# The second part's products by quarters: seven products instead of eight, with sums on GpSimd

## The chip, the cores and the metric

One NeuronCore of a Trainium2 chip runs the whole program. Its engines work in parallel, each through its own queue in a fixed order: TensorE (PE, with its weight loads shown apart as PEld), VectorE (DVE), ScalarE (ACT), GpSimd (POOL), and SyncE (SP), which here only issues DMAs. The metric is the device time of one execution in microseconds, as the median of some runs.

## The reference

Attention over chunks gives `x` (3072 tokens, 512 wide). Two dense parts follow; the change is in the second.

```python
# first part: 512 -> 2048 -> 512
h = x @ w_in
x = (np.maximum(h, 0.0) + alpha * np.minimum(h, 0.0)) @ w_out
# second part: 512 -> 1536 -> 512
a = x @ w_a
b = x @ w_b
return (a * b @ w_o2).astype(np.float32)
```

The weights arrive as 64-bit floats. Attention works on 32 queries at a time with a few neighbours and 8 memory rows for each of 8 heads.

## The kernel before

TensorE multiplies in float16. Each operand is split into a high and a low half (`split_hi` on ACT, `split_lo` on DVE), and `gemm3` makes three matmuls of each product: high by high, high by low, low by high. Each matmul loads its own 128x128 weights.

In the first part, attention units of 128 tokens feed blocks of tokens (two of 256, five of 512). Of each block, `gemm1` and `gemm2` are worked one after the other, and the result goes to DRAM as `yd`. Beside this, `chunk` turns the 64-bit words of `w_a`, `w_b` and `w_o2` into scaled halves in the tile `sp`, and stores them in DRAM (`wa_d`, `wb_d`, `w_d`): 12 chunks of 1024 columns and 8 of 768.

In the second part, `second` runs for six blocks of 512 tokens. It loads `yd`, finds the largest value (`scale`, which crosses the partitions with a small PE transpose), and splits. `one_product` makes, 12 times in a block, two products of 4 x 3 matmuls of 512 columns. ACT takes the first out of PSUM (line 1109), DVE multiplies the second by it (1114, tile `p32`) and finds its size (1120). After another `scale`, ACT and DVE split the 12 tiles (339, 343) into `phl`, and `output` makes four products of 12 x 3 matmuls of 512 columns (evacuated in line 1148, stored in 1156). So a block has 288 + 144 = 432 matmuls. `w_a`, `w_b` and `w_o2` are loaded once into the space of the first part's weights, and stay there. There are eight PSUM banks (`mm` and `mm2`, four each).

The order of all queues is fixed when the program is built. `Schedule.emit` takes, again and again, the operation that can start first by costs written in the code (`pe`, `dve`, `act`, `dma`), and among equals the one of the lowest rank. In the second part block `jb` has rank 3000 + 20 `jb`, its outputs 30 more, and what empties PSUM 1000 less. So PE works the first products of block `jb` + 1 before the outputs of block `jb`, which come while the next block's splits are made.

Of the kernel before, what the change touches and what calls it, by code (L numbers as in the profile page):

```python
# [56 lines left out]
class Schedule:  # L57
# [43 lines left out]
    def start(self, o, free):  # L101
# [3 lines left out]
        for b in o.bufs.values():  # L105
            if not b.held:
                s = b.slots
                k = need.get(id(s), 0)
                if len(s.free) <= k or (s.in_order and s.waiting[k] is not b):
                    return None  # L110
                t = max(t, s.free[k] + (self.DMA_LAG if o.engine == "SP" else 0.0))
                need[id(s)] = k + 1
        return t

    def emit(self):
# [6 lines left out]
        for _ in range(len(self.ops)):  # L122
# [25 lines left out]
            for b in o.bufs.values():  # L148
                b.users -= 1
                if not b.users and b.slots is not None:  # L150
                    b.slots.free.append(o.end + self.LAG[e])
                    b.slots.free.sort()
# [18 lines left out]
def act(n, pointers=0):  # L171
    return 0.06 + 0.09 * pointers + n * 0.833 / 1000

# [6 lines left out]
def tile_attention_moe_moe2(  # L180
# [33 lines left out]
    NC2 = DF2 // CW  # L214
    NR = DM // CR
    GR = CW // P
# [28 lines left out]
    def col(n=1):  # L245
# [14 lines left out]
    inv_w = {  # L260
        "wa": col(NC2),
        "wb": col(NC2),
        "w3": col(NR),
    }
    inv_cols = const.tile([P, NR, CR], F32, name="inv_cols")

# [6 lines left out]
        nm: dram.tile([P, n], F16, name=f"{nm}_d")  # L273
        for nm, n in (("wa", 2 * KD * DF2), ("wb", 2 * KD * DF2), ("w3", 2 * KF2 * DM))
# [21 lines left out]
    def scale(amax, s, inv, reads, writes, rank=-2000, after=()):  # L296
# [16 lines left out]
        def inverse():  # L313

            nc.vector.tensor_scalar(inv, m.tile, TINY, 1.0 / TOP, op0=ALU.max, op1=ALU.mult)
# [31 lines left out]

    xhl_slots = slots(actp, 1, [P, 2, KD, TB], F16, "xhl")
    ghl_slots = slots(actp, 1, [P, 2, KF1, TB], F16, "ghl")
    raw_slots = slots(prep, 3, [P, 1024, 2], I32, "raw")  # L350
    ah_slots = slots(prep, 1, [P, 1024], BF16, "ah", in_order=False)
    w32_slots = slots(prep, 2, [P, 1024], F32, "w32")
    sp_slots = slots(prep, 1, [P, 2, 1024], F16, "sp")

    def halves(t, kt):

        return t.rearrange("p (x k f) -> x p k f", x=2, k=kt)
# [40 lines left out]
    def chunk(nm, c, w, kt, cw, rank, load_rank):  # L398
        cols = slice(c * cw, (c + 1) * cw)
        n = kt * cw  # L400
        raw = None if nm == "w1" else Buf(raw_slots)
        rk = raw_key(c) if nm == "w1" else (raw, 0)
        ah, w32 = (None, "w32w1") if nm == "w1" else (Buf(ah_slots), Buf(w32_slots))
# [4 lines left out]
        def load():  # L408
            load_words(raw_tile(c) if nm == "w1" else raw.tile, w, kt, cols)
# [44 lines left out]
        def sizes():  # L454

            nc.scalar.activation(
                out=ah.tile[:, :n], in_=w32.tile[:, :n], func=ACTF.Abs, accum_out=am
            )
# [21 lines left out]
        if nm != "w1":  # L480
            sd.op("ACT", act(n, 2), rank, sizes, [fk], [(ah, 0), (key + "am", 0)])
# [4 lines left out]
        def scaled():  # L486
# [17 lines left out]
            else:  # L504
                sp = Buf(sp_slots)

                def hl():
                    t = sp.tile[:, :, :n]
                    return t[:, 0], t[:, 1]

                def hi_():
                    split_hi(w32.tile[:, :n], hl()[0], s)

                def lo_():
                    split_lo(w32.tile[:, :n], *hl(), s)

                def store():
                    nc.sync.dma_start(
                        out=spill[nm][:, 2 * n * c : 2 * n * (c + 1)].rearrange("p (x n) -> p x n", x=2),
                        in_=sp.tile[:, :, :n],  # L520
                    )

                sd.op("ACT", act(n, 1), rank, hi_, src, [(sp, 0)])
                sd.op("DVE", dve(n, pointers=1), rank, lo_, src + [(sp, 0)], [(sp, 1)])
                sd.op("SP", dma(n * 4 * P), rank, store, [(sp, 0), (sp, 1)], [(key, 0)])
# [416 lines left out]
    for nm, w, kt, cw in (("wa", w_a, KD, CW), ("wb", w_b, KD, CW), ("w3", w_o2, KF2, CR)):  # L942
        for c in range(w.shape[1] // cw):
            chunk(nm, c, w, kt, cw, 1000 + c, 1000 + c)


# [5 lines left out]

    late = {}

    def slots2(pool, count, shape, dtype, name, in_order=True):
        return Slots(
            count,
            lambda: pools2[pool].tile(shape, dtype, tag=name, name=name, bufs=count),
            in_order,
        )  # L960

    def w1_again():
        late["w1"] = wpool.tile([P, 2 * KD * DF1], F16, tag="w1", name="w1b")

    def w2_again():
        late["w2"] = wpool.tile([P, 2 * KF1 * DM], F16, tag="w2", name="w2b")

    sd.op("PE", 0.0, 0, w1_again, (), [(f"w1{c}", 0) for c in range(NC1)] + [("w1b", 0)])
    sd.op("PE", 0.0, 0, w2_again, (), [(f"w2{c}", 0) for c in range(NR)] + [("w2b", 0)])
    phase1 = [("att", i) for i in range(len(units))] + [  # L970
        (f"{nm}{c}", 0) for nm, n in (("wa", NC2), ("wb", NC2), ("w3", NR)) for c in range(n)
# [4 lines left out]
    n = 2 * KD * CW  # L976
    where = {}
    order = [("wa", 0), ("wb", 0), ("wa", 1), ("wb", 1)] + [("wa", c) for c in range(2, NC2)]
    for i, key in enumerate(order):
        where[key] = ("w1", i)  # L980
    for c in range(2, NC2):
# [224 lines left out]
```

## Time and profile before

| | |
|---|---|
| median of 3 runs | 1247.84 us (1247.73 to 1250.45) |
| profiled execution | 1250.38 us, of which the span is 1248.6 |
| mean granted TensorE clock | 0.997 |
| busy in the span | PE 1190.5, PEld 621.2, DVE 672.3, ACT 520.5, POOL 5.0 us |
| matmuls | 7362 recorded |

Busy time of PE is modelled: each matmul is shown longer than the distance to the next, so the distance of starts tells its pace. POOL is used only for masks at the start. In the profile's view by slices, DVE is nine tenths busy in most of the first third and two to three tenths later; PE is full from there to the end, at the full clock.

### The profile page before, as it was taken

Reading aid. Unit: us, or ns where it says so; the run is one execution under the profiler, and the core shown is the slowest. Engines: PE = TensorE matmul, PEld = TensorE weight load, DVE = VectorE, ACT = ScalarE, POOL = GpSimd, SP = SyncE. Lnnn points to the kernel's source line nnn. Section 1 sums busy time; section 2 is a strip of 40 time slices with the busy share of each in tenths; the row PEclk is TensorE's granted clock in tenths of the full one; section 3 lists DMA queues with packets and bytes.
Section 4 is the critical chain, followed back from the end, with each engine's and each line's share of the span. In section 5 each row is a group of like instructions: output and inputs, shape, how many; then the busy total and the mean of one; then the engine's idle time right before and its main releaser. Section 6 shows DMA issues by size and latency. Waiting matters only on the chain.

```text
span 1248.6 us, 18309 instructions
## 1 busy us (share of the span) xinstructions
PE 1190.5 (95%) x7362; PEld 621.2 (50%) x7362; DVE 672.3 (54%) x1225; ACT 520.5 (42%) x1204; POOL 5.0 (0%) x41
## 2 busy tenths in 40 slices
PE   4399999999999999999999999999999999999998
PEld 3278885555555544444444444444444444444443
DVE  6979998988888653252341536352342342232330
ACT  4679778866886672260450223221221221121120
POOL 1000000000000000000000000000000000000000
PEclk9999999999999999999999999999999999999999
DMA  8954776568447204101031301010000000000000
GB/s 236 267 115 101 192 187 184 143 194 238 120 123 180 66 1 113 48 1 56 12 140 64 134 1 34 1 68 1 1 34 1 1 34 1 1 35 1 1 34 34
DMA packets 157796, 99.76 MB, mean 80 GB/s; under 512 B 102912, under 2 KB 134672, under 8 KB 157712
## 3 DMA queue, kind: packets, MB, share of 16 engines
q1 hardware_dynamic: 157712, 98.59, 27.7%
q8 instruction: 58, 0.95, 0.3%
q14 instruction: 26, 0.21, 0.1%
HBM read 76.55 MB, written 22.02 MB: 79 GB/s over the span
## 4 chain that ended last, share of the span: by engine, by line
PE 76%; DVE 13%; ACT 6%; DMA 2%; issue 2%; SPq 1%; ACTq 0%; DVEq 0%
PE mm L799 24%; PE mm L801 24%; PE mm L800 24%; DVE w L443 2%; ACT sm L655 2%; PE pair L681 1%; DVE w L450 1%; DVE g L822 1%; DVE ghl L831 1%; DVE sp L343 1%; PE mm L695 1%; DVE nm L645 1%; DVE w L436 1%; DVE columns L704 1%; DVE sm L635 1%
## 5 line engine op out<-in xcount | busy, mean ns | idle before, releaser
L1109 ACT ACTIVATE t<-mm,columns 128x512 f32<-128x512 f32 x72 | 49.4, 686 | 404.8 <-PE mm L801 401.2
L1114 DVE SCALAR_TENSOR_TENSOR p<-mm,columns,t 128x512 f32<-128x512 f32 x72 | 54.0, 750 | 242.0 <-PE mm L801 234.5
L801 PE MATMUL mm<-xhl,w 128*128 128x512 f16 (+1 forms) x448 | 157.7, 352 | 1.9 <-DVE w L443 1.9
L800 PE MATMUL mm<-xhl,w 128*128 128x512 f16 (+1 forms) x448 | 157.8, 352 | 0.2 <-DVE xhl L343 0.2
L799 PE MATMUL mm<-xhl,w 128*128 128x512 f16 (+1 forms) x448 | 157.9, 352 | 0.1
L801 PE MATMUL mm<-ghl,w 128*128 128x512 f16 (+1 forms) x448 | 156.6, 350 | 0.5 <-DVE w L343 0.5
L799 PE MATMUL mm<-ghl,w 128*128 128x512 f16 (+1 forms) x448 | 156.8, 350 | 0.0
L800 PE MATMUL mm<-ghl,w 128*128 128x512 f16 (+1 forms) x448 | 156.7, 350 | 0.0
L801 PEld LDWEIGHTS <-w 128*128 128x128 f16 x896 | 88.3, 99 | 83.0 <-DVE w L443 2.2
L799 PEld LDWEIGHTS <-w 128*128 128x128 f16 x896 | 88.7, 99 | 75.5 <-issue 0.6
L800 PEld LDWEIGHTS <-w 128*128 128x128 f16 x896 | 88.3, 99 | 73.6 <-issue 0.8
L816 ACT ACTIVATE g<-mm 128x512 f32<-128x512 f32 (+1 forms) x112 | 59.9, 540 | 86.6 <-PE mm L801 83.7
L822 DVE SCALAR_TENSOR_TENSOR g<-t,columns,g 128x512 f32<-128x512 f32 (+1 forms) x112 | 74.6, 671 | 32.4 <-ACT t L819 32.1
L831 DVE TENSOR_TENSOR ghl<-g,ghl 128x512 f16<-128x512 f32 (+1 forms) x112 | 67.6, 610 | 29.8 <-ACT ghl L828 29.6
L828 ACT CAST ghl<-g 128x512 f16<-128x512 f32 (+1 forms) x112 | 62.1, 562 | 37.7 <-DVE g L822 37.5
L800 PE MATMUL mm<-w2b,w1b 128*128 128x512 f16 x192 | 72.8, 379 | 0.0
L799 PE MATMUL mm<-w2b,w1b 128*128 128x512 f16 x192 | 72.8, 379 | 0.0
L799 PE MATMUL mm<-xhl,w1b 128*128 128x512 f16 x192 | 72.8, 379 | 0.0
L801 PE MATMUL mm<-xhl,w1b 128*128 128x512 f16 x192 | 72.8, 379 | 0.0
L801 PE MATMUL mm<-w2b,w1b 128*128 128x512 f16 x192 | 72.8, 379 | 0.0
L800 PE MATMUL mm<-xhl,w1b 128*128 128x512 f16 x192 | 72.8, 379 | 0.0
L1148 DVE SCALAR_TENSOR_TENSOR g<-mm,columns,inv_cols 128x512 f32<-128x512 f32 x24 | 18.0, 748 | 100.5 <-PE mm L801 100.5
(134 smaller groups left out, 1988.4 us busy)
## 6 DMA issues: line engine op xcount, KB each, us to landing
raw<-in_moe_w_out_dram SPq DMA_DIRECT2D x8, 1024.0 KB
kw<-in_k_dram SPq DMA_DIRECT2D x40, 176.0 KB
vw<-in_v_dram SPq DMA_DIRECT2D x40, 176.0 KB
qt<-in_q_dram SPq DMA_DIRECT2D x24, 256.0 KB
raw<-in_moe_w_a_dram SPq DMA_DIRECT2D x6, 1024.0 KB
raw<-in_moe_w_b_dram SPq DMA_DIRECT2D x6, 1024.0 KB
raw<-in_moe_w_out_dram SPq DMA_DIRECT2D x8, 768.0 KB
out_dram<-g SPq DMA_DIRECT2D x24, 256.0 KB
```

What stands on the lines that cost most here:

```text
L443: nc.vector.scalar_tensor_tensor(out=f, in0=lo, scalar=29, in1=f, op0=ALU.logical_shift_right, op1=ALU.bitwise_or)
L655: nc.scalar.activation(out=sm.tile[:, o, g], in_=scored()[:, o, g], func=ACTF.Exp, bias=stat["nm"][:, i : i + 1], scale=1.0, accum_out=sta ...
L799: nc.tensor.matmul(out=ps, lhsT=lh, rhs=rh, start=first and i == 0, stop=False)
L800: nc.tensor.matmul(out=ps, lhsT=lh, rhs=rl, start=False, stop=False)
L801: nc.tensor.matmul(out=ps, lhsT=ll, rhs=rh, start=False, stop=last and i == n - 1)
L816: nc.scalar.activation(out=g.tile[:, :n], in_=ps.tile[:, :n], func=ACTF.Relu, scale=E1)
L822: nc.vector.scalar_tensor_tensor(out=g.tile[:, :n], in0=t2.tile[:, :n], scalar=nal[:, m : m + 1], in1=g.tile[:, :n], op0=ALU.mult, op1=ALU ...
L828: nc.scalar.copy(out=ghl.tile[:, 0, m, d], in_=g.tile[:, :n])
L831: nc.vector.tensor_tensor(out=ghl.tile[:, 1, m, d], in0=g.tile[:, :n], in1=ghl.tile[:, 0, m, d], op=ALU.subtract,)
L1109: nc.scalar.activation(out=a.tile, in_=pa.tile, func=ACTF.Copy, scale=iab["wa"][:, c : c + 1])
L1114: nc.vector.scalar_tensor_tensor(out=p32.tile, in0=pb.tile, scalar=iab["wb"][:, c : c + 1], in1=a.tile, op0=ALU.mult, op1=ALU.mult,)
L1148: nc.vector.scalar_tensor_tensor(out=o.tile, in0=ps.tile, scalar=io, in1=inv_cols.rearrange("p c f -> p (c f)"), op0=ALU.mult, op1=ALU.mult,)
```

## The change

The operands of the second part are cut in quarters. With two sums or differences of quarters per operand set, a product of two by two quarters takes seven products of quarters (`SEVEN`) instead of eight; the results are put together by additions. What that changes in the program:

- A unit is a block of rows by 2x2 quarters: four quarters of 256 columns and three made of them ("others"). The four sums of a unit are GpSimd instructions of 128x256 (`sums`, line 367 of the changed kernel). Then ACT and DVE split 1024 and 768 columns (`split_unit`, line 351 on DVE).
- `w_a`, `w_b` and `w_o2` are prepared in 18 units of 1024 columns; seven quarters in two halves of each are stored, 917,504 bytes.
- `pair` takes the place of two `one_product`: 2 x 7 products of 2 x 3 matmuls of 256 columns, six times in a block. `output` makes 7 products of 6 x 3 matmuls of 256 columns, twice in a block. That is 504 + 252 = 756 matmuls.
- `quarters` takes seven products out of four PSUM banks: two ACT instructions (256 and 512 columns), three on DVE (256, 512, 256; lines 409, 427, 433), and two on GpSimd (256 and 768; lines 418 and 421). DVE's 512 wait for GpSimd's 768.
- For each pair DVE multiplies 1024 columns (line 1295) and finds their size (line 1301). GpSimd makes the sums of the six units of this product and of the next block's two units of `y`.
- `w_a` and `w_b` are no longer kept. They stream through four places of a unit each (`ring_slots`): 12 units in the first block, 8 in every later one, which walks the other way.
- In the last block the sums of the product's units may go to DVE too.

```diff
+def pool(n):
+    return 0.1 + n * 2.2 / 1000
+    SEVEN = {1: (0, 0), 6: (5, 5), 5: (4, 4), 7: (2, 2), 3: (6, 3), 4: (3, 6), 2: (1, 1)}
+    def sums(rank, u, o, reads, writes, steps, cost={"POOL": pool(HT)}):
+        for out_, i, x, a, y, b, op in steps:
+            def f(e="POOL", out_=out_, i=i, x=x, a=a, y=y, b=b, op=op):
+                (nc.vector if e == "DVE" else nc.gpsimd).tensor_tensor(
+                    out=out_()[:, i], in0=x()[:, a], in1=y()[:, b], op=op
+                )
+            sd.op("POOL", cost, rank, f, reads, [(u, "sum"), (o, "sum")] + writes)
...
+        y, x, z, w = Buf(mm_slots), Buf(mm2_slots), Buf(mm2_slots), Buf(mm_slots)
+        half = {1: (y, 0), 6: (y, 1), 5: (x, 0), 7: (x, 1), 3: (z, 0), 4: (z, 1), 2: (w, 0)}
...
+        sd.op("ACT", act(HT, 1), er, first, [(y, 0)], [(c, 0)])
+        sd.op("DVE", dve(HT, pointers=1), er, add_sixth, [(y, 1), (c, 0)], [(u, 0)])
+        sd.op("ACT", act(TB, 1), er, fifth_seventh, [(x, 0), (x, 1)], [(c, 1)])
+        sd.op("POOL", pool(HT), er, c22, [(c, 1)], [(c, 3)])
+        sd.op("POOL", pool(3 * HT), er, add_all, [(u, 0)], [(c, 1), (c, 3)])
+        sd.op("DVE", dve(TB, pointers=1), er, add_third_fourth, [(z, 0), (z, 1)], [(c, 1)])
+        sd.op("DVE", dve(HT, pointers=1), er, add_second, [(w, 0)], [(c, 0)])
...
+        for j in js:
+            pair(jb, j, here, yu, ps[j], iab, amp, r)
...
+        pu = {j: Buf((ring_slots if i < 4 else yu_slots) if last_ else pu_slots) for i, j in enumerate(js)}
+        cost = {"POOL": pool(HT), "DVE": dve(HT)} if last_ else {"POOL": pool(HT)}
+        for j in js:
+            operands(r, ps[j], pu[j], lambda j=j: spj[:, j : j + 1], [(f"sp{jb}", 0), (ps[j], 0)], cost)
```

DVE's queue in the second part of the kernel before, while a middle block's products are made; the outputs named `ghl` are splits of the block before:

```order
L1114 SCALAR_TENSOR_TENSOR p32_7645<-mm2_7584,columns_84,t2_7597 128x512
L343 SCALAR_TENSOR_TENSOR ghl_7624<-p32_7276,columns_84,ghl_7624 128x512
L1120 TENSOR_REDUCE columns_84<-p32_7645 128x1
L343 SCALAR_TENSOR_TENSOR ghl_7624<-p32_7315,columns_84,ghl_7624 128x512
L1114 SCALAR_TENSOR_TENSOR p32_7667<-mm2_7630,columns_84,t2_7643 128x512
L343 SCALAR_TENSOR_TENSOR ghl_7624<-p32_7347,columns_84,ghl_7624 128x512
L1120 TENSOR_REDUCE columns_84<-p32_7667 128x1
```

The same place of DVE's queue in the changed kernel (a middle block's pairs; `cb` holds the second product, `x32_6480` and `ghl_7244` here are places of units):

```order
L409 SCALAR_TENSOR_TENSOR g_9178<-mm_9179,cb_9177 128x256
L351 SCALAR_TENSOR_TENSOR ghl_7244<-x32_6480,columns_84,ghl_7244 128x1024
L433 SCALAR_TENSOR_TENSOR cb_9177<-mm_9231,cb_9177 128x256
L409 SCALAR_TENSOR_TENSOR g_9241<-mm_9242,columns_84,x32_6480 128x256
L351 SCALAR_TENSOR_TENSOR ghl_7244<-s32_9141,columns_84,ghl_7244 128x768
L427 SCALAR_TENSOR_TENSOR cb_9177<-mm2_9212,cb_9177 128x512
L1295 SCALAR_TENSOR_TENSOR ghl_7244<-cb_9177,columns_84,ghl_7244 128x1024
L433 SCALAR_TENSOR_TENSOR x32_6480<-mm_9294,columns_84,x32_6480 128x256
L1301 TENSOR_REDUCE columns_84<-ghl_7244 128x1
```

Where two instructions per product stood with a split between them, there are now three per seven products, with splits and the multiplication among them, and line 427 stands behind line 433 though its products are made first: it waits for GpSimd.

GpSimd's queue at that place of the changed kernel; in the kernel before there is nothing in it after the masks:

```order
L418 TENSOR_TENSOR cb_9177<-cb_9177 128x256
L367 TENSOR_TENSOR w1b_7012<-w1b_7012 128x256
L421 TENSOR_TENSOR cb_9177<-cb_9177,g_9178 128x768
L367 TENSOR_TENSOR s32_9219<-s32_9219,w1b_7012 128x256
L367 TENSOR_TENSOR s32_9219<-w1b_7012,s32_9219 128x256
L418 TENSOR_TENSOR x32_6480<-x32_6480 128x256
L367 TENSOR_TENSOR s32_9301<-xhl_7034 128x256
L421 TENSOR_TENSOR x32_6480<-x32_6480,g_9241 128x768
```

The sums of the block before (line 367) stand between the additions that empty PSUM (418 and 421).

DVE's queue in the first part of the kernel before, at its first chunk of `w_a`:

```order
L343 SCALAR_TENSOR_TENSOR sp_2397<-w32_2104,columns_84,sp_2397 128x1024
L666 RECIPROCAL rs_2428<-rs_2428 128x8
L450 SCALAR_TENSOR_TENSOR w32_2262<-raw_1963,w32_2262 128x1024
L671 TENSOR_TENSOR sm_2279<-sm_2279,rs_2428 128x384
L865 TENSOR_SCALAR g_2467<-mm_2381,columns_84 128x256
```

And in the changed kernel:

```order
L351 SCALAR_TENSOR_TENSOR sp_2392<-w32_2098,columns_84,sp_2392 128x1024
L777 RECIPROCAL rs_2424<-rs_2424 128x8
L351 SCALAR_TENSOR_TENSOR sp_2392<-raw_1912,columns_84,sp_2392 128x768
L782 TENSOR_TENSOR sm_2279<-sm_2279,rs_2424 128x384
L976 TENSOR_SCALAR g_2462<-mm_2376,columns_84 128x256
```

A second split of 768 columns has come in for each chunk; the order of attention and evacuations around it is nearly as before.

## Rows read from the trace of the kernel before

**Rows 1.** Busy us by stretch: PE, PEld, DVE, ACT, POOL, clock, DMA share, GB/s.

```profile
100.00:400.00 300.00, 286.37 (x2640) 184.67 (x2639) 272.76 (x556) 237.12 (x635) 0.00 (x0) 1.00 0.63 170
400.00:450.00 50.00, 49.73 (x350) 26.85 (x349) 34.07 (x66) 33.33 (x98) 0.00 (x0) 1.00 0.15 49
684.00:1244.50 560.50, 560.50 (x2603) 254.92 (x2602) 199.21 (x318) 106.81 (x164) 0.00 (x0) 1.00 0.07 23
640.00:660.00 20.00, 20.00 (x95) 9.09 (x93) 6.89 (x10) 6.00 (x11) 0.00 (x0) 1.00 0.75 276
```

**Rows 2.** Waits from 684 us to the end: total us, times, longest.

```profile
ACT t L1109 <- PE mm L801: 401.2, 67, 40.1
DVE p L1114 <- PE mm L801: 234.5, 63, 4.5
```

**Rows 3.** Timeline around the second part's edges: start us, us, engine, line.

```profile
683.99 0.38 PE L801 MATMUL mm<-ghl,w 128*128 128x512 f16 x1
684.21 0.38 PE L799 MATMUL mm<-xhl,w1b 128*128 128x512 f16 x1
...
1244.52 0.38 PE L801 MATMUL mm<-w,phl 128*128 128x512 f16 x1
1244.94 0.75 DVE L1148 SCALAR_TENSOR_TENSOR g<-mm,columns,inv_cols 128x512 f32<-128x512 f32 x1 [7.02 <-PE mm L801]
```

**Rows 4.** Timeline of PE in the second part, 512 columns.

```profile
955.19 0.38 PE L800 MATMUL mm<-w2b,w1b 128*128 128x512 f16 x1
...
958.43 0.38 PE L800 MATMUL mm<-w2b 128*128 128x512 f16 x1
```

**Rows 5.** Timeline of PE and PEld in the first part's 256-column blocks.

```profile
100.14 0.27 PE L800 MATMUL mm<-xhl,w 128*128 128x256 f16 x1
...
103.97 0.27 PE L799 MATMUL mm<-xhl,w 128*128 128x256 f16 x1
...
103.97 0.10 PEld L800 LDWEIGHTS <-w 128*128 128x128 f16 x1
```

**Rows 6.** Groups of DVE by form: names, shapes, count, busy us, mean ns, idle before.

```profile
L1114 DVE SCALAR_TENSOR_TENSOR p<-mm,columns,t 128x512 f32<-128x512 f32 x72 | 54.0, 750 | 242.0 <-PE mm L801 234.5 <-ACT w2b L339 7.4
L1120 DVE TENSOR_REDUCE columns<-p 128x1 f32<-128x512 f32 x72 | 49.3, 685 | 2.2
L343 DVE SCALAR_TENSOR_TENSOR sp<-w,columns,sp 128x1024 f16<-128x1024 f32 x12 | 15.3, 1278 | 2.5 <-ACT sp L339 2.4
L822 DVE SCALAR_TENSOR_TENSOR g<-t,columns,g 128x256 f32<-128x256 f32 x32 | 14.9, 478 | 3.2 <-ACT t L819 3.1
L831 DVE TENSOR_TENSOR ghl<-g,ghl 128x256 f16<-128x256 f32 x32 | 12.8, 417 | 1.2 <-ACT ghl L828 1.1
L343 DVE SCALAR_TENSOR_TENSOR sp<-w,columns,sp 128x768 f16<-128x768 f32 x8 | 8.1, 1016 | 6.4 <-ACT sp L339 6.4
L1051 DVE TENSOR_REDUCE columns<-x 128x1 f32<-128x2048 f32 x3 | 6.8, 2280 | 12.0 <-DMA x<-yd 12.0
```

**Rows 7.** Timeline of DVE, five instructions of one line in a row.

```profile
759.55 3.39 DVE L343 SCALAR_TENSOR_TENSOR ghl<-p,columns,ghl 128x512 f16<-128x512 f32 x5
```

**Rows 8.** Groups of POOL: names, shapes, count, busy us, mean ns.

```profile
L279 POOL CAST ident<-ident 128x128 bf16<-128x128 f32 x1 | 0.3, 289 | 0.1
L1190 POOL MEMSET const-float32-0.0<- 128x1 f32 x1 | 0.1, 103 | 0.2 <-issue 0.2
```

**Rows 9.** Groups of ACT by form, columns as in rows 6.

```profile
L339 ACT ACTIVATE sp<-w,columns 128x1024 f16<-128x1024 f32 x12 | 13.8, 1147 | 8.7 <-DMA wb_d<-sp 6.4 <-DMA wa_d<-sp 2.3
L1109 ACT ACTIVATE t<-mm,columns 128x512 f32<-128x512 f32 x72 | 49.4, 686 | 404.8 <-PE mm L801 401.2 <-issue 3.5
```

**Rows 10.** Timeline of DVE at the last block's second `scale`.

```profile
1184.24 0.17 DVE L1079 TENSOR_REDUCE columns<-columns 128x1 f32<-128x12 f32 x1
...
1187.03 4.07 DVE L343 SCALAR_TENSOR_TENSOR phl<-p,columns,phl 128x512 f16<-128x512 f32 x6 [0.79 <-ACT phl L339]
```

More of the change, by code (lines that the diff above doesn't have):

```diff
@@ L37, in __init__, with add @@
         self.waiting = []
+    def add(self, t, places):
+        self.free += [(t, p) for p in places]
+        self.free.sort(key=lambda x: x[0])
 class Buf:
@@ L951, in start2 @@
         pools2["ps"] = ctx.enter_context(tc.tile_pool(name="mm2", bufs=4, space=PSUM))
[L953 to L960, printed above, removed]
+        us = units_of(pools2["act"].tile([P, 8 * UN], F16, tag="units", name="units"), 8)
+        w3_slots.add(sd.now, us[:NJ])
+        yu_slots.add(sd.now, us[NJ:])
@@ L972, in tile_attention_moe_moe2 @@
     ]
     sd.op("PE", 0.0, 0, start2, phase1 + [("alpha", 0)], [("act2", 0)])
[L976 to L981, printed above, removed]
-        where["wb", c] = ("w2", c - 2)
-    order += [("wb", c) for c in range(2, NC2)]
-    def w_ab(nm, c):
-        t, i = where[nm, c]
-        return late[t][:, i * n : (i + 1) * n]
-    for i, (nm, c) in enumerate(order):
+    passes = []
@@ new lines, in tile_attention_moe_moe2, with load @@
+    last = {}
+    for jb in range(NB2):
+        js = range(NJ) if jb % 2 == 0 else range(NJ - 1, -1, -1)
+        here = {}
+        for i, j in enumerate(js):
+            for nm in ("wa", "wb"):
+                if i < 2 and jb:
+                    here[nm, j] = last[nm, j]
+                    continue
+                here[nm, j] = b = Buf(ring_slots)
+                def load(nm=nm, j=j, b=b):
+                    nc.sync.dma_start(
+                        out=b.tile.rearrange("p x o f -> p (x o f)"),
+                        in_=spill[nm][:, j * UN : (j + 1) * UN],
+                    )
+                sd.op("SP", dma(UN * 2 * P), 2000 + 20 * jb + 2 * i, load, [(f"{nm}{j}", 0)], [(b, 0)])
+        last = here
+        passes.append((js, here))
@@ new lines, in output, with product, reads, store @@
+    def output(jb, tt, pu, io, r):
+        c = Buf(cb_slots)
+        d = slice(tt * P, (tt + 1) * P)
+        def product(i, out_):
+            a, b = SEVEN[i]
+            gemm3(
+                out_,
+                [
+                    tuple(pu[j].tile[:, x, a, d] for x in range(2))
+                    + tuple(w3u[j].tile[:, x, b] for x in range(2))
+                    for j in pu
+                ],
+            )
+        def reads(i):
+            a, b = SEVEN[i]
+            return NJ * pe(HT, 3), [(pu[j], a // 4) for j in pu] + [(w3u[j], 0) for j in pu]
+        quarters(r, r - 1000, c, Buf(g_slots), product, lambda: io, reads)
+        row = jb * TB + tt * P
+        for h in range(2):
+            def store(h=h):
+                nc.sync.dma_start(
+                    out=out[row + h * HT : row + h * HT + P, :],
+                    in_=c.tile[:, 2 * h : 2 * h + 2].rearrange("p o f -> p (o f)"),
+                )
```

421 lines of the change are left out of this document (245 added, 176 removed).

## The prediction

> **What bounds the kernel now.** I read the busy time by stretch first, then the waits, then single rows of the timeline. From 684 us on, PE is busy for all of 560.5 us at the full clock, while DVE is busy for 199 and ACT for 107 [rows 1]. The waits say the same from the other side: ACT and DVE wait for PE's matmuls, 401 and 234 us, and no wait of PE is among them [rows 2]. The second part begins when the last matmul of the first part has gone, at 684.2, and its last matmul starts at 1244.5; one evacuation and one store follow, about 4 us [rows 3]. So the second part is a row of matmuls without a gap, and its time is their count by their pace: 15 starts lie between 955.19 and 958.43, 0.216 us each [rows 4]; 2592 of these are 560 us. In the first part it is otherwise: from 100 to 400 us PE is busy for 286 of 300 and DVE for 273 [rows 1]; both are near their limit there, and from 400 to 450 DVE has 16 of 50 us free.
>
> **What the change removes.** A block has 756 matmuls of 256 columns instead of 432 of 512, which is seven eighths of the columns. The pace of 256 columns stands in the first part: 35 starts from 100.14 to 103.97, 0.1094 us each, and a weight load of 0.10 us still fits under each [rows 5]. So 6 x 756 x 0.1094 = 496.2 us against 560.5: **-64.3**, if PE never waits. A block is then 504 x 0.1094 = 55.1 us of pairs and 27.6 us of outputs; seven products of a pair's half are 42 x 0.1094 = 4.6 us.
>
> **What it adds beside PE.** The order shows where it falls: while the pairs of one block are made, GpSimd makes the sums of the block before (its units' places come free only when the outputs before them are done) and of the next `y`; DVE makes all their splits there too. So the pairs' 55.1 us have to hold, per block:
>
> DVE. A row's time minus 0.08 is its step, since five of the 0.75 us instructions take 3.39 us, 0.66 each [rows 7]. Emptying PSUM: 12 x (0.40 + 0.67 + 0.40) = 17.6, from 478 and 750 ns. The multiplication of 1024 columns: 6 x 1.20 = 7.2, priced as a split of 1024. Sizes of 1024 columns, a third of the way from 685 ns (512) to 2280 (2048): 1.14, 8 of them 9.1. Splits: 8 x (1.20 + 0.94) = 17.1. All from [rows 6]; with 2 us for two `scale` chains it is **53.0 of 55.1**.
>
> GpSimd. No row shows it add two tensors. It casts 128 columns in 289 ns and sets one column in 103 [rows 8]: 1.48 ns a column for one input. If two inputs come together, 256 columns take 0.48 us and 768 take 1.24; if they come one after the other, 0.86 and 2.37. (DVE's 417 ns for 256 columns [rows 6] lies just below these.) I take the middle, 0.67 and 1.80, there being no row nearer to one end. Then 12 x (0.67 + 1.80) + 32 x 0.67 = **51.1 of 55.1**, with ends 36.0 and 66.3.
>
> ACT has 24 evacuations of at most 0.69 and 16 splits of at most 1.15 [rows 9], at most 35 us: hidden. The stream of weights costs nothing: 8 units of 0.92 MB, a block of `y` and one of the output are 9.4 MB in 82.7 us, 114 GB/s, where 276 GB/s were moved at three quarters of the DMA's time [rows 1]; the four places hold two pairs, 18 us. Were this cover gone, a unit would come 3.3 us late.
>
> **The wait it adds.** DVE's line 427 waits for GpSimd's 768 columns, and DVE's queue is strict: behind it stand the next halves' evacuations, the multiplication and the splits, and PE waits for the banks. Two sets of banks take up one set of products, 4.6 us of lateness in a stage; the outputs' 27.6 us, with 3 us of evacuation and 5 of GpSimd, let both engines catch up before the next stage. So a stage costs what DVE or GpSimd need over 55.1 + 4.6 = 59.7.
>
> Alone, neither is over. But both read SBUF: of DVE's 53 us, 7.2 + 17.1 = 24.3 are instructions with two SBUF inputs. Whether these and GpSimd's get in each other's way no row of before can show, because GpSimd is idle beside them; the ends are no collision, 0, and none at once, all 24.3. For want of a nearer row I take the half, 12.2 us of waiting in DVE's queue: 65.2 against 59.7, 5.5 us in four stages. In the last block there is no next `y` (7.6 us less): nothing. In the first there are no sums of a block before: nothing. **+22**.
>
> The SBUF — State Buffer page of the Trainium skill, section "Who interferes with whom", has a rule against this change: a DVE instruction with two SBUF inputs and a GpSimd instruction that reads SBUF exclude each other for their whole length. No run here shows it yet; it is the first rival below.
>
> The GPSIMD Engine Reference of the Trainium skill, section "Elementwise — side-by-side cycle accounting", gives 4497 ns for an addition of 2048 columns, by which I estimate 0.56 us for 256 and 1.69 for 768. With these the stage on GpSimd would be 45 us, and the sum below the same, since DVE sets it; no row of before has this operation.
>
> **The first part.** 18 units are split 1024 + 768, 18 x 2.294 = 41.3 us on DVE, where 12 x 1.278 + 8 x 1.016 = 23.5 were: +17.8. GpSimd gets 72 x 0.67 = 48 us; half of that as collisions is 24 on DVE. From 100 to 450 us DVE has 350 - 306.9 = 43.1 us free [rows 1], just the sum of both. It isn't free where it is wanted: ACT's splits now wait for four sums in a row, and attention is queued behind them. Ends 0 and 17.8 + 48 - 43.1 = 23; I take **+10**.
>
> **The end.** The last block's chain is covered by the outputs of the one before, 27.6 us. From the last product to the first split it was 2.8 us after the sizes [rows 10]; evacuation, multiplication and sizes come ahead with 0.40 + 0.67 + 1.20 + 1.14, then 14 sums on DVE (0.34 each, from 417 ns), six splits (12.8) and two evacuations (2.9): 26.7 plus the waits between DVE and GpSimd. Ends 0 and 12; I take **+6**, with what the second part's beginning may lose.
>
> **Sum.** The profiled execution took 1250.4 (span 1248.6 and 1.8 around it): 1250.4 - 64.3 + 22 + 10 + 6 = 1224. It is 2.5 us above the median of the runs, so the forecast is **1222**.
>
> **Rivals.**
>
> *One at a time.* If DVE's two-input instructions and GpSimd's sums exclude each other wholly, a stage needs 51.1 + 24.3 = 75.4, 15.7 over, four times, and in the last block 51.1 - 5.4 + 20.0 = 65.7, 6 over: 69. The first part loses its 23, the end 10: 1250.4 - 64.3 + 69 + 23 + 10 = 1288, at the median 1286: slower. The mechanism is the queue behind line 427, in the pairs of blocks 1 to 5. It turns into a loss when a stage's sum of both exceeds about 70 us. With GpSimd's lower price it is 60.3, and the time 1206. For it: two inputs of a column in one step of about 1.1 ns have to be read from somewhere [rows 6]. Against it: no row shows a shared path.
>
> By the page's price for GpSimd and its rule together the stage would be 45 + 24.3 = 69.3 and the time about 1246, no change; both pages are those named above.
>
> *No collision.* Then DVE and GpSimd fit their 55.1 us, and only 3 us in the first part and 4 at the end are lost: 1250.4 - 64.3 + 7 = 1193, at the median 1191. For it: neither engine is over by its own rows. Against it: 53.0 and 51.1 of 55.1 leave nothing for a queue that waits for another.
>
> *GpSimd dear.* At 0.86 and 2.37 without collisions a stage is 66.3, four times 6.6 over, 26 us instead of 22: inside the forecast. With collisions it is over 1340.
>
> **Chances.** The forecast 0.38, one at a time 0.40 at all prices (0.29 of it slower), no collision 0.18, dear with collisions 0.04. The forecast's own range is 1205 to 1244. One at a time as a whole is a little likelier, but it is spread from 1206 to 1286, and the forecast lies at its lower middle. The range is 1192 to 1290; 0.08 are left out on either side. A measurement of this kernel can tell about 0.3%, 3.7 us, from no change: faster 0.35 + 0.18 + 0.05 = 0.58, same 0.03 + 0.06 = 0.09, slower 0.29 + 0.04 = 0.33.
>
> **What would show it.** PE's starts in the second part 0.109 us apart wherever it runs, and its idle time there, none now, 20 to 30 us, put down to DVE, and in the pairs of blocks 1 to 4, not in the outputs. GpSimd's 256 columns near 0.67 us. If DVE's splits grow from 1.28 us beside GpSimd, or GpSimd's 768 columns beside them, they collide; if DVE is over 65 us busy or waiting in a pairs' stage it is the first rival. The end of the first part, now at 684, should lie near 694. Wrong would be: PE idle in the outputs, a wait of PE for the weights' stream, or a clock below 0.99 in the second part, which I count on staying at the full level.

## The result, and the profile after

The changed kernel took **1264.09 us** (median of 4 runs, 1262.69 to 1265.76) against 1249.14 (1247.73 to 1250.88) for the kernel before on the same chip: a ratio of 1.012, interval 1.0097 to 1.0142. It is slower by 1.2 per cent, where 1222 and faster were forecast. The profiled execution took 1262.69, of which the span is 1260.9, 12.3 us more than before.

Where the 12.3 us lie is read from three rows of PE's timeline (start us, us, engine, line), which answer to [rows 3].

```profile
689.83 0.38 PE L912 MATMUL mm<-ghl,w 128*128 128x512 f16 x1
690.04 0.27 PE L910 MATMUL mm<-units,w1b 128*128 128x256 f16 x1
...
1257.05 0.27 PE L912 MATMUL mm<-units 128*128 128x256 f16 x1
```

The second part begins at 690.04 instead of 684.21 (+5.8), and its starts span 567.0 us instead of 560.3 (+6.7); the tail is as before. So the 64.3 us of matmuls are saved, and 70.8 come back inside the second part (567.0 against 496.2 by count). The busy time by stretch shows where; the columns are those of [rows 1].

```profile
100.00:400.00 300.00, 284.30 (x2611) 182.47 (x2610) 269.56 (x515) 238.82 (x625) 54.18 (x56) 0.99 0.60 167
400.00:450.00 50.00, 48.42 (x304) 25.62 (x302) 43.09 (x79) 36.94 (x98) 9.79 (x11) 0.97 0.51 168
690.00:745.00 55.00, 55.00 (x505) 49.26 (x504) 38.55 (x49) 16.46 (x28) 34.60 (x26) 1.00 0.43 139
838.00:907.00 69.00, 58.69 (x502) 50.44 (x500) 53.77 (x66) 24.27 (x37) 58.78 (x50) 0.93 0.40 130
907.00:935.00 28.00, 28.00 (x259) 25.06 (x258) 14.88 (x20) 5.80 (x8) 14.82 (x13) 1.00 0.06 20
```

The first block's pairs (690 to 745) and the outputs of the middle blocks (28 us) run without a gap. From the second block on a pairs' stage takes longer: by PE's starts 64.7, 69.5, 70.4, 69.1 and 63.1 us instead of 55.1, together 61 us. There GpSimd is busy for 58.8 us and DVE for 53.8 of 69, and the clock's mean is 0.93. PE, which waited for nothing before [rows 2], now does. Its waits from 690 us on, and DVE's (what waits, for whom: total us, times, longest):

```profile
PE mm L910 <- DVE cb L427: 24.3, 7, 4.6
PE mm L310 <- DVE columns L1235: 16.0, 3, 5.5
PE mm L912 <- DVE units L351: 5.4, 2, 3.0
```

```profile
DVE cb L427 <- POOL cb L421: 36.1, 20, 2.7
```

PE waits for banks that DVE's line 427 empties; DVE waits there for GpSimd's line 421; and at three blocks PE stands at the transposition of the next `y`'s sizes (line 310). PE's timeline of one stall, which answers to [rows 4, 5], shows a second price:

```profile
872.69 0.27 PE L912 MATMUL mm<-units,w1b 128*128 128x256 f16 x1
877.60 0.28 PE L910 MATMUL mm<-units,w1b 128*128 128x256 f16 x1 [4.64 <-DVE cb L427]
877.72 0.27 PE L911 MATMUL mm<-units,w1b 128*128 128x256 f16 x1
877.83 0.37 PE L912 MATMUL mm<-units,w1b 128*128 128x256 f16 x1
877.99 0.42 PE L910 MATMUL mm<-units,w1b 128*128 128x256 f16 x1
878.20 0.42 PE L911 MATMUL mm<-units,w1b 128*128 128x256 f16 x1
...
897.73 0.47 PE L310 MATMUL mm<-ident,columns 128*128 128x128 f32 x1 [5.55 <-DVE columns L1235]
898.00 0.42 PE L910 MATMUL mm<-units,w1b 128*128 128x256 f16 x1
898.21 0.42 PE L911 MATMUL mm<-units,w1b 128*128 128x256 f16 x1
```

Before the stall the starts are 0.109 apart, the pace of [rows 5]; 0.4 us behind it they come to be 0.213 apart, for some 3 us, and again behind the next one: the lower of the two clocks, 1.2 GHz. The window from 877 to 881 us, half a microsecond of it still standing, has a granted clock of 0.61:

```profile
877.00:881.00 4.00, 3.40 (x18) 2.39 (x19) 4.00 (x6) 1.51 (x2) 3.92 (x5) 0.61 0.00 0
```

In the second part some 160 matmuls have this pace, 34.5 us instead of 17.5. So the 70.8 us are about 34 of waiting in the products (6 of them before the last outputs), 20 at the transpositions (18 of them waiting), and 17 of half clock. (The mean clock of a run doesn't tell this price: the profiled run, at 0.958, has 0.73 and 0.83 in its first two stretches of 50 us, where PE is busy for 24 and 36 us; another of the four has 0.977 and the same span, 1261.2.)

Why DVE and GpSimd are late is seen instruction by instruction, in the same 5 us of both engines: first DVE, then GpSimd.

```profile
962.02 1.81 DVE L1295 SCALAR_TENSOR_TENSOR xhl<-cb,columns,xhl 128x1024 f32<-128x1024 f32 x1
963.75 0.47 DVE L433 SCALAR_TENSOR_TENSOR w2b<-mm,columns,w2b 128x256 f32<-128x256 f32 x1
964.15 1.20 DVE L1301 TENSOR_REDUCE columns<-xhl 128x1 f32<-128x1024 f32 x1
965.27 0.41 DVE L409 SCALAR_TENSOR_TENSOR g<-mm,cb 128x256 f32<-128x256 f32 x1
965.61 2.34 DVE L351 SCALAR_TENSOR_TENSOR ghl<-quarters,columns,ghl 128x1024 f16<-128x1024 f32 x1
```

```profile
962.02 0.73 POOL L367 TENSOR_TENSOR s<-quarters,s 128x256 f32<-128x256 f32 x1
962.71 1.71 POOL L418 TENSOR_TENSOR w2b<-w2b 128x256 f32<-128x256 f32 x1
964.37 0.73 POOL L367 TENSOR_TENSOR s<-x 128x256 f32<-128x256 f32 x1
965.06 1.81 POOL L421 TENSOR_TENSOR w2b<-w2b,g 128x768 f32<-128x768 f32 x1
966.83 1.71 POOL L367 TENSOR_TENSOR x<-x 128x256 f32<-128x256 f32 x1
```

Follow the hand-over. GpSimd's sum takes 0.73 from 962.02; DVE's multiplication, issued with it, ends at 963.83, 1.08 after GpSimd's end at 962.75, where 1024 columns alone take 1.28 [rows 6]: they begin in the last 0.2 us of the sum as it is recorded. GpSimd's next sum, issued at 962.71, ends at 964.42, 0.59 after DVE's, of the 0.73 that it takes alone. Then DVE reads one input (lines 433, 1301, 409: one from PSUM, or one in all), and both engines keep their own times, 0.73 and 1.20. From 965.06 GpSimd has its 768 columns, 1.81; DVE's split, issued at 965.61, ends 1.08 after them; and GpSimd's next sum, issued at 966.83, ends 0.59 after that. An instruction of DVE with two SBUF inputs and a sum of GpSimd run one behind the other, but for 0.1 to 0.2 us, and the one that waits is the one that came later.

By groups the same is read as two means. GpSimd's from 690 us on, to be set against 0.73 and 1.81 above (these answer to [rows 8], where it had nothing of this kind):

```profile
L421 POOL TENSOR_TENSOR cb<-cb,g 128x768 f32<-128x768 f32 x48 | 100.1, 2086 | 22.0 <-DVE g L409 20.1
L418 POOL TENSOR_TENSOR cb<-cb 128x256 f32<-128x256 f32 x48 | 52.7, 1099 | 86.6 <-ACT cb L415 84.9 <-DVE w2b L351 1.5
```

DVE's split of 768 columns, 1016 ns in [rows 6], and an evacuation, which is not lengthened:

```profile
L351 DVE SCALAR_TENSOR_TENSOR ghl<-s,columns,ghl 128x768 f16<-128x768 f32 x20 | 31.0, 1551 | 0.0
L409 DVE SCALAR_TENSOR_TENSOR g<-mm,cb 128x256 f32<-128x256 f32 x36 | 14.8, 412 | 3.1 <-ACT cb L406 3.1
```

Both engines pay. From 838 to 907 us GpSimd's 49 additions take 60.4 us, where they take 47.7 at 0.73 and 1.81; DVE's 17 splits and multiplications take 29.5 instead of 20.1. The larger part falls on GpSimd, and that is the engine to which the lateness leads back: from 840 to 880 us its additions are over four fifths of the chain that ended last.

With the prices now measured, a pairs' stage has 12 x (0.73 + 1.81) + 32 x 0.73 = 53.8 us of GpSimd and 24.3 of DVE that exclude each other, 78 us of a shared way where 59.7 can be held.

### The profile page after: what moved, and what is told of

Its sections match the earlier page's. It is cut to its first block, busy times and chain, and to the rows that moved or that the text cites. A ratio compares the mean times of both kernels' runs of the same rounds, so it can differ in the third digit from the quotient of the medians.

```text
span 1260.9 us, 23247 instructions
## 1 busy us (share of the span) xinstructions
PE 1149.2 (91%) x9304; PEld 818.7 (65%) x9304; DVE 894.0 (71%) x1415; ACT 606.0 (48%) x1320; POOL 492.9 (39%) x459
## 4 chain that ended last, share of the span: by engine, by line
PE 34%; DVE 22%; POOL 21%; issue 10%; ACT 6%; SPq 4%; DMA 2%; POOLq 0%; ACTq 0%; DVEq 0%
PE mm L910 10%; PE mm L912 10%; PE mm L911 10%; POOL s L367 7%; POOL cb L421 5%; DVE ghl L351 2%; DVE ghl L942 2%; DVE g L933 2%; SPq L688 2%; POOL cb L418 2%; DVE w L553 1%; DVE sp L351 1%; ACT sm L766 1%; PE pair L792 1%; POOL xhl L367 1%
## 5 line engine op out<-in xcount | busy, mean ns | idle before, releaser
L910 PE MATMUL mm<-units,w1b 128*128 128x256 f16 x560 | 156.4, 279 | 9.7 <-DVE cb L427 9.6
L367 POOL TENSOR_TENSOR raw<-w 128x256 f32<-128x256 f32 x18 | 14.6, 808 | 377.8 <-ACT raw L568 215.4
L910 PE MATMUL mm<-w2b,w1b 128*128 128x256 f16 x504 | 142.0, 282 | 16.7 <-DVE cb L427 14.7
L911 PE MATMUL mm<-units,w1b 128*128 128x256 f16 x560 | 156.3, 279 | 0.0
L912 PE MATMUL mm<-units,w1b 128*128 128x256 f16 x560 | 156.0, 279 | 0.0
L911 PE MATMUL mm<-w2b,w1b 128*128 128x256 f16 x504 | 141.8, 281 | 0.0
L912 PE MATMUL mm<-w2b,w1b 128*128 128x256 f16 x504 | 141.6, 281 | 0.0
L910 PEld LDWEIGHTS <-w1b 128*128 128x128 f16 x1064 | 107.2, 101 | 42.8 <-DVE cb L427 26.6
L911 PEld LDWEIGHTS <-w1b 128*128 128x128 f16 x1064 | 107.0, 101 | 16.7 <-issue 1.7
L912 PEld LDWEIGHTS <-w1b 128*128 128x128 f16 x1064 | 107.0, 101 | 15.0
L421 POOL TENSOR_TENSOR cb<-cb,g 128x768 f32<-128x768 f32 x48 | 100.1, 2086 | 22.0 <-DVE g L409 20.1
```

The costliest lines, as they stand in the source:

```text
L367: (nc.vector if e == "DVE" else nc.gpsimd).tensor_tensor(out=out_()[:, i], in0=x()[:, a], in1=y()[:, b], op=op)
L421: nc.gpsimd.tensor_tensor(out=c.tile[:, 1:4], in0=c.tile[:, 1:4], in1=u.tile[:, None, :HT].to_broadcast([P, 3, HT]), op=ALU.add,)
L910: nc.tensor.matmul(out=ps, lhsT=lh, rhs=rh, start=first and i == 0, stop=False)
L911: nc.tensor.matmul(out=ps, lhsT=lh, rhs=rl, start=False, stop=False)
L912: nc.tensor.matmul(out=ps, lhsT=ll, rhs=rh, start=False, stop=last and i == n - 1)
```

## The experiments

The theory, "one at a time": the two exclude each other wholly, and what is late on DVE's queue holds up PE. Rivals: DVE's or GpSimd's own time, the chain of the evacuations itself, or the transpositions that stand in PE's queue. Each kernel is the changed one with the edit shown; ratios are against the kernel before, on the same chip.

**e1: the instructions stay, but DVE reads one input.** The splits' second halves and line 1295's multiplication, in the second part, are given one input with the same columns, so the values are others.

```diff
+                    nc.vector.tensor_scalar(
+                        hl()[:, 1, places], f(), s(), -1e30, op0=ALU.mult, op1=ALU.max, accum_out=junk
+                    )
...
-            nc.vector.scalar_tensor_tensor(
-                out=p32.tile, in0=cb.tile, scalar=iab["wb"][:, j : j + 1], in1=p32.tile,
...
+            nc.vector.tensor_scalar(
+                p32.tile, cb.tile, iab["wb"][:, j : j + 1], -1e30, op0=ALU.mult, op1=ALU.max,
```

> In the second part DVE's low halves of the splits and its multiplication become instructions with one SBUF input and the same columns (what they compute is changed; about 1.21 us for 1024, as the first part's instruction of that kind). Theory 'one at a time' (DVE's two-input instructions and GpSimd's sums exclude each other): GpSimd's 256 columns take 0.73 us and its 768 take 1.81 throughout, the pairs' stages fall from 63-70 us to 55-57, PE's clock stays at full, and the time is 1195 to 1210. Rival 'GpSimd too slow' (its own 54 of 55 us and DVE's strict queue behind it): stages stay at 63 us or more, 1250 to 1264. Rival 'transposes in PE's queue' (PE stands at the next y's scale because DVE is late): the waits of 5 us at the transposes stay, 1245 to 1264.

1197.59 us (1194.49 to 1198.87), ratio 0.9567 (0.9543 to 0.959). The stages are 54.9 to 55.4 us. Groups of GpSimd and of DVE in it:

```profile
L427 POOL TENSOR_TENSOR cb<-cb,g 128x768 f32<-128x768 f32 x48 | 87.2, 1817 | 2.5
L424 POOL TENSOR_TENSOR cb<-cb 128x256 f32<-128x256 f32 x48 | 34.9, 728 | 112.3 <-ACT cb L421 112.3
```

```profile
L384 DVE TENSOR_SCALAR_CACHE_REDUCE ghl<-s,columns 128x768 f16<-128x768 f32 x20 | 20.1, 1003 | 0.0
L1301 DVE TENSOR_SCALAR_CACHE_REDUCE xhl<-cb,columns 128x1024 f32<-128x1024 f32 x10 | 12.8, 1276 | 0.2
```

The same columns at DVE's price of before, and GpSimd's sums at their price alone. Neither engine's own time binds, the stands at the transpositions are gone too, and with the second input go 66.5 us. (The splits then no longer read ACT's halves either; in the changed kernel DVE's waits for these are 5.6 us.) That is the cause, shown.

**e2: the next `y`'s scale waits for the block before's sizes of p.** Nothing is left out here, nor in e3 and e4.

```diff
-        scale(lambda: am1y, s, inv, [(f"amy1{jb}", 0)] + known, ...
+        scale(lambda: am1y, s, inv, [(f"amy1{jb}", 0)] + known + ([(f"amp1{jb - 1}", 0)] if jb > 1 else []), ...
```

> From the third block on, y's scale waits for the largest product of the block before, so that its transposes, sums and splits fall in the outputs' stage. 'One at a time': a stage loses 8 sums x 0.73 and 4.3 us of splits, 10 us of its 78 on the shared way, so four stages get 8 to 10 us shorter, and the time is 1215 to 1230. 'GpSimd too slow': the stage keeps 48 us of GpSimd and DVE's waits, 1245 to 1255. 'Transposes in PE's queue': the 16 us of waits at the transposes go with the half clock behind them, about 1235, and the other stall of 5 us in each stage stays as it is.

1249.8 us (1247.04 to 1253.0), ratio 0.9991 (0.9976 to 1.0007). The expectation was missed. The stand of 16.0 us for the next `y`'s sizes (line 310) went, and 14 us with it, but PE's wait for line 427 stayed whole, and 7.0 us of waiting for p's own sizes came, where 1.5 were:

```profile
PE mm L910 <- DVE cb L427: 23.9, 7, 4.6
PE mm L310 <- DVE columns L1250: 7.0, 6, 1.9
```

The stages are 63.1 to 63.8 us. That one stand goes and the other stays is what the rival of the transpositions had said, though with 1235 us. So it doesn't do to hold a stage's sum against its length: in the stage from 835 to 898 us, 23 of the p units' 24 sums stand in the first 44 us, and PE's stand of 4.6 us lies there, 35 us behind the stage's beginning.

**e3: line 418's addition on DVE, out of PSUM.** It then has one input in SBUF.

```diff
-            nc.gpsimd.tensor_tensor(out=c.tile[:, 3], in0=c.tile[:, 1], in1=c.tile[:, 2], op=ALU.add)
+            nc.vector.scalar_tensor_tensor(
+                out=c.tile[:, 3], in0=bank(x)[:, 1], scalar=scale_of(), in1=c.tile[:, 1],
+                op0=ALU.mult, op1=ALU.add,
+            )
```

> The fourth quarter's first addition (256 columns, 14 in a block) goes from GpSimd to DVE, reading the seventh product out of PSUM, so with one SBUF input. 'One at a time': 12 x 0.73 = 8.8 us less on the shared way of a stage, 69 instead of 78, while DVE gets 4.8 us more (58 of 55): 1225 to 1240. If it is DVE's own time that binds, it gets slower: 1265 to 1285. 'Transposes in PE's queue': unchanged within 5 us.

1232.79 us (1230.84 to 1234.8), ratio 0.9857 (0.9831 to 0.9883): as expected. DVE has 12 instructions of 0.41 us more in a stage, and it became shorter: 59.5 to 60.7 us.

**e4: e2 and e3 together.**

> The two edits together: y's scale later, and the fourth quarter's first addition on DVE. 'One at a time': 78 - 10 - 9 = 59 us on the shared way of a stage, within the 59.7 that it can hold: stages of 55 to 58 us, 1198 to 1212. If DVE's own time binds: about 1235. If GpSimd's own time binds: as with one edit alone, 1230.

1223.72 us (1220.01 to 1224.37), ratio 0.9773 (0.9748 to 0.9798): 12 us over what was expected, with stages of 59 to 61 us, though the shared way was put at 59, within the 59.7. PE still waits some 2.5 us once a stage, at the same place:

```profile
PE mm L913 <- DVE xhl L430: 4.9, 3, 2.5
PE mm L913 <- DVE ghl L430: 2.5, 1, 2.5
PE mm L913 <- DVE w1b L430: 2.5, 1, 2.5
PE mm L913 <- DVE quarters L430: 2.5, 1, 2.5
```

**e5: without the p operands' sums.** The changed kernel; the other three operands are taken from the unit's own quarters.

```diff
-        others = lambda: o.tile
+        others = lambda: unit()[:, :3] if leave else o.tile
...
+        if leave:
+            split_unit(r, b, unit, b, others, h, lambda: h.tile, s, reads)
+            return
```

> Leaves out the four sums of each p operand unit (24 of GpSimd's additions of 256 columns in a block); the unit's own quarters stand in for the other three quarters, so the products are other numbers. Splits, matmuls, evacuations and their sums stay. One at a time, where the sums stand: a pairs' stage needs 12 x 2.53 + 8 x 0.73 + 24.3 = 60.6 us of the shared way instead of 78.1, against 59.7 that it can hold, and nothing of GpSimd stands beside the first five pairs but the evacuations' own sums: stages 55 to 58 us, gaps of 3 us at most, no half clock, 1202 to 1215 us. Rival, the delay comes from the evacuations' own chain (the additions of lines 418 and 421, which stay): the gaps of 4.9 us stay and the time is over 1240.

1208.43 us (1207.75 to 1209.47), ratio 0.9662 (0.9646 to 0.9679), as expected, with stages of 56.2 to 56.7 from the third block on; the second block's stays at 63.8, with a stand of 3.4 us at the next `y`'s transposition and half clock behind it. The additions of the evacuations (lines 418 and 421) are all there; the rival, that their chain holds up PE, fails: its wait fell from 24.3 us to 6.7.

```profile
PE mm L910 <- DVE cb L427: 6.7, 6, 1.5
```

**e6: the output by eight products again.** The two products of the pairs stay at seven; the output has 144 matmuls of 512 columns in a block, and neither p nor `w_3` needs sums. Nothing is left out.

```diff
-            operands(r, ps[j], pu[j], ..., cost)
-        for tt in range(HT // P):
+            split_unit(
+                r, ps[j], lambda j=j: ps[j].tile, ps[j], None, pu[j], ..., four=True,
+            )
+        for tt in range(TB // P):
```

> The two products that make a pair stay at seven quarters; the output's product goes back to eight, 144 matmuls of 512 columns in a block (31.1 us instead of 27.6), so neither p's operands nor w_3's need sums or splits of the other three quarters. PE by its count: 6 x (55.1 + 31.1) = 517.4 us. One at a time: the shared way has 12 x 2.53 + 8 x 0.73 for GpSimd and 7.2 + 4.6 + 7.7 for DVE, 55.7 us in a stage that holds 59.7: stages 55 to 58, with the first part 3 us and the end 3 us over before: 1207 to 1218 us, faster than the change although PE has 21 us more to do. Rival, what costs is the evacuations' chain itself: stages of 65 and over, 1250 to 1270.

1217.07 us (1214.07 to 1218.57), ratio 0.9728 (0.9706 to 0.9749): PE has 21 us more to do than in the changed kernel, and it is 47 us faster.

**e7: e6 with the edits of e2 and e3.**

> The same with the addition of line 418 on DVE out of PSUM and with the next y's scale behind the block before's p. One at a time: the shared way falls by 12 x 0.73 to 47, and no stage was over, so at most the few us that the kernel without these two edits still loses come back: 1203 to 1215, 0 to 6 under it. Rival, DVE's own time (12 x 0.40 more, 20 splits less): no sign of it, since it stays under 52 us.

1210.11 us (1208.2 to 1211.86), ratio 0.9675 (0.9656 to 0.9694). PE has no wait at all in its second part; the windows' columns are as above:

```profile
686.00:1204.00 518.00, 518.00 (x3900) 381.26 (x3898) 334.24 (x518) 135.25 (x200) 160.35 (x106) 1.00 0.32 106
```

**e8: e4 with p's sums on DVE or GpSimd.**

```diff
-        cost = {"POOL": pool(HT), "DVE": dve(HT)} if last_ else {"POOL": pool(HT)}
+        cost = {"POOL": pool(HT), "DVE": dve(HT)}
```

> The kernel with both edits (line 418 on DVE, y's scale later), and p's sums on DVE or GpSimd in every block, as the planner's times have it, instead of GpSimd alone. One at a time: a sum takes 0.34 us of the shared way on DVE instead of 0.73 on GpSimd, so with all 24 moved the way in a stage is 12 x 1.81 + 8 x 0.73 + 24.3 + 24 x 0.34 = 60.1 instead of 69.3: 1205 to 1216 us. Rival, DVE's own queue: DVE then has 53 + 4.8 + 8.2 = 66 us in a stage that holds 59.7: stages of 61 to 66, 1225 to 1245, slower than with GpSimd alone (1223.7).

1234.2 us (1231.28 to 1237.03), ratio 0.9869 (0.9841 to 0.9897): 10 us slower than e4, as the rival had it. But its stages are 58.8 us, not longer than e4's. Only some of the sums moved (one stage has 5 of them on DVE and 17 on GpSimd), and what came instead is a stand of up to 2.4 us before the outputs, at p's own scale:

```profile
PE mm L310 <- DVE columns L1253: 9.4, 5, 2.4
```

With this stand, and half clock behind it at two blocks, the outputs take 29.9 to 32.0 us instead of 27.7 to 28.6, and there the 10 us lie. Why p's scale comes later is not settled.

**e10: sums made early.** e4 with a third place for their results; the first p unit's sums (in the second kernel the first two units') are made while the outputs before still hold the unit's own place.

```diff
-        sd.op("POOL", 0.0, r, lambda: None, reads, [(h, "held")], holds=[h])
+        if not early:
+            sd.op("POOL", 0.0, r, lambda: None, reads, [(h, "held")], holds=[h])
...
+                early=i < 1 and jb > 0 and not last_,
```

> The kernel with both edits (line 418 on DVE, y's scale later; 1223.7 us, stages 58.9 to 60.7), a third place for the sums' results, and the sums of the first p unit of each block but the first and last made before the unit's own place is free: they then stand beside the outputs, where GpSimd is idle, instead of beside the first pairs. Nothing is left out. One at a time, where the sums stand: 4 x 0.73 = 2.9 us of the shared way leave the pairs' stage of four blocks, and what they delay at its crowded beginning: stages 56 to 58, 1209 to 1218 us. Rival, the delay in mid-stage comes from DVE's own time: nothing changes, 1220 to 1227.

> The same with the first two p units: 5.8 us leave the stage. One at a time: 55.5 to 57.5 us a stage, 1204 to 1216. Rival, the two units keep two of the three places until the outputs end, so the next y's units go through one place, one behind the other: PE then stands before the pairs' first product, 2 to 4 us a block, and the time is 1215 to 1230, not under that with one unit.

One unit: 1218.19 us (1216.21 to 1219.94), ratio 0.9733 (0.9706 to 0.976), stages of 57.4 from the fourth block on, at the expectation's upper end. Two units: 1230.93 (1230.29 to 1232.57), ratio 0.9832 (0.9809 to 0.9855): the rival's time, but its mechanism only in part. PE stands before the pairs' first products once, 6.3 us at the third block; the later stages, of 59.8 us, have four short waits for banks instead of two, and the rival had not named these.

**e9 and e12: the planner told the true prices.** e9 is e4, e12 the changed kernel, with costs raised (the line with `c22` is e12's alone).

```diff
-            sd.op("DVE", dve(n, pointers=1), rank, lo_, ...
+            sd.op("DVE", dve(n, pointers=1) + 0.5, rank, lo_, ...
...
-        sd.op("POOL", pool(HT), er, c22, [(c, 1)], [(c, 3)])
-        sd.op("POOL", pool(3 * HT), er, add_all, [(u, 0)], [(c, 1), (c, 3)])
+        sd.op("POOL", pool(HT) + 0.35, er, c22, [(c, 1)], [(c, 3)])
+        sd.op("POOL", pool(3 * HT) + 0.3, er, add_all, [(u, 0)], [(c, 1), (c, 3)])
...
-            cost,
+            {e: c + 0.35 if e == "POOL" else c for e, c in cost.items()},
```

> The kernel with both edits; only the planner's costs change, to what the trace shows beside the other engine: a split's second half + 0.5 us on DVE, GpSimd's sums + 0.35 (256 columns) and + 0.3 (768). The work is the same and so is the sum of the shared way, so one at a time expects little: another order, 1212 to 1226 us. Rival, the loss is one of order (the planner believes in 0.66 us where 1.4 are taken, and so puts DVE's work in a wrong order): under 1212.

> The changed kernel as it is, with the planner's costs alone raised to what the trace shows beside the other engine: a split's second half + 0.5 us on DVE, the additions of lines 367 and 418 + 0.35, that of line 421 + 0.3. If the loss is the shared way itself, the order matters little, since the work in a stage is the same: 1250 to 1268 us (the change: 1264). Rival, a good part of the loss is the order made from too low costs (evacuations put behind splits that the planner thought short, and the 5 us stalls with their half clock): 1230 to 1250.

e9 took 1222.06 us (1220.67 to 1224.02), ratio 0.9761 (0.9731 to 0.979), as expected, and no other time than e4: its second part begins 6 us earlier, at 683.4, and takes 4 more. Yet its stages are 54.9 us without a gap from the third block on. The lateness has only moved: PE now stands before the outputs, for the last split of p, and mostly has half clock behind it.

```profile
PE mm L915 <- DVE ghl L351: 20.9, 6, 4.1
```

e12 took 1243.02 us (1238.38 to 1246.36), ratio 0.9944 (0.9925 to 0.9963): 21 us under the changed kernel with no instruction less, so the rival has its part. Its stages are 54.9 us from the third block on, too, and PE stands at p's scale, up to 10.5 us in front of the next outputs:

```profile
PE mm L310 <- DVE columns L1250: 44.4, 5, 10.5
```

Of the 21 us, 6 lie in the first part, which e1 left as it was: the second begins at 683.9 instead of 690.0. So of the 66 us that the collisions cost in the second part, some 15 come from the order made without them, and the rest stays under this order too: it shows at another place.

**e11: e9 with one unit's sums early.**

> The kernel with both edits (line 418 on DVE, y's scale later), the raised planner's costs (whose pairs' stages were without a gap, 54.9 us, but PE stood 3.5 us before each outputs and ran at half clock behind it), and the first p unit's sums made early into a third place. One at a time: 2.9 us of sums leave the stage, so the 3.5 us before the outputs shrink to under 1 and the half clock behind them goes, some 5 us a block: 1198 to 1210 us. Rival, the early unit only takes the y's place and the stand before the outputs stays: 1218 to 1226.

1203.32 us (1202.79 to 1203.93), ratio 0.9631 (0.9606 to 0.9657), as expected; nothing is left out, and it is faster than both kernels. Of its 61 us under the changed kernel, 12 lie in the first part (the second begins at 678.3); 5 of these it has over e9, with the same costs, and no run explains them. Two of its blocks, pairs and outputs, without a gap and at the full clock; 82.7 us each by count:

```profile
824.90:907.70 82.80, 82.80 (x761) 74.23 (x760) 68.78 (x101) 29.91 (x44) 58.86 (x47) 1.00 0.35 115
907.70:990.60 82.90, 82.90 (x761) 74.15 (x759) 67.55 (x99) 28.62 (x43) 58.34 (x46) 1.00 0.35 115
```

## Why the prediction was wrong

**The step that failed** is "For want of a nearer row I take the half", of the 24.3 us of DVE's two-input instructions. There is no half: the rows at 962 to 967 us show the whole, and e1, without the second input, is within 7 us of the 1191 that "no collision" was given. The first rival named the mechanism, the queue behind line 427, and its size for the stages: 15.7 us over in four and 6 in the last, 69; measured were 9.6, 14.4, 15.3, 14.0 and 8.0, 61. It was given the greater chance in the text's own words, but the forecast was put beside it, on a value for which no row spoke.

The half was also laid on one engine alone, as waiting in DVE's queue. In the stage from 838 to 907 us, 9 us of waiting are DVE's and 13 GpSimd's, 22 together; GpSimd, at 51.1 of 55.1 us by the prediction's own sum, had no room for its part. That the rival's 69 lie so near the 61 is in part luck: its sum has neither the transpositions nor the half clock, which are some 30 us of the 61, and e2 shows that a stage is not as long as its sum.

The SBUF — State Buffer page of the Trainium skill, section "Who interferes with whom", which the prediction weighed and set aside as a rival, says just this of DVE with two SBUF inputs and GpSimd. The traces agree in each row read, but for the 0.1 to 0.2 us above, also in that an evacuation with one input from PSUM keeps its 0.41 us.

The other steps, one by one:

- PE's count and pace, -64.3: right. The starts are 0.109 us apart; e7's second part, 518.0 us without a gap, is its count as well.
- GpSimd's price, 0.67 and 1.80 for 256 and 768 columns: 0.73 and 1.81, a little dearer (its 1.48 ns a column is 1.46 by its own rows, which changes nothing). The estimate from the GPSIMD Engine Reference of the Trainium skill, section "Elementwise — side-by-side cycle accounting", 0.56 and 1.69, was low by nearly a quarter and by a fifteenth.
- "The outputs' 27.6 us let both engines catch up": right for the middle blocks, whose outputs have no gap.
- DVE's 53.0 us fit by themselves: right by e1.
- The first part, +10 with ends 0 and 23: 5.8. DVE's busy time from 100 to 400 us is 269.6 where it was 272.8; the added work came later, from 400 to 450 us (43.1 instead of 34.1), into the free time that the prediction saw there, and from 450 to 680 (100.7 instead of 86.1), where it had not looked. The 24 us of collisions that it laid on DVE fell mostly on GpSimd: its 72 sums took 70.9 us instead of 52.6 at 0.73, DVE's 36 splits 42.9 instead of 41.3. A part of the 5.8 is order, for with e12's costs the second part begins at 683.9. The rival's 23 were wrong, which is the largest part of why the time is 22 us under its 1286.
- The end, +6: about 8. Two gaps of 3.3 and 2.8 us before the last outputs, and half clock behind them.
- Not foreseen: PE standing at the next `y`'s transposition, 16 us (e2 takes it away), and the clock. The prediction counted on the full level, and named a clock below 0.99 as a sign of being wrong; it is 0.95 from 690 us on, and fell behind each stall of about 5 us.
- The stage's sum against 59.7 us was too smooth a picture: what is late depends on where in the stage the sums stand (e2, e10) and on the order that the planner made from costs without collisions (e12).

## What to carry to other kernels

Moving work to an idle engine is not free where both engines read the same memory: add up the instructions that exclude each other as if they were one engine's, and look for forms that don't (one operand out of PSUM, or one input only). A planner that schedules by costs must be given the price beside the other engine, or it can put the critical evacuation behind an instruction that it believes short; here that alone gave 21 us in the changed kernel (e12), and nothing in e4 (e9). And a saving need not be taken whole: seven products for the two products whose sums fit, eight for the third, was 47 us faster than the changed kernel (e6). Seven for all was faster than that only with line 418 on DVE, `y` later, the true prices and early sums together (e11, 1203 against e7's 1210).

## What the runs showed of the hardware

- GpSimd adds two f32 tensors of 256 columns in 0.73 us and of 768 in 1.81, if nothing stands in its way: 2.1 ns a column, three quarters more than DVE's price for the same 256 columns (0.417 [rows 6]).
- An instruction that waits for the other engine in this way is shown as busy, not as waiting: a DVE split of 1024 columns reads 2.34 us instead of 1.28. In the busy times alone the collision looks like work; only single rows beside the other engine's tell.
- PE, held up for 4.64 us in the middle of a product, ran at half clock for about 3 us soon after. Behind all seven stands of 4.6 to 5.6 us in the changed kernel's second part its starts were 0.213 us apart for 2.8 to 5.5 us, and behind one of two of 2.7 us.
